# Loading the first batch's q in two token halves, one ahead of v and one behind it

## The chip, the cores and the metric

The kernel runs on one core of one Trainium2 chip. The metric is device time in microseconds of one execution, the median over several; lower is better. Two kernels are compared by a ratio, with a 95% interval, in the same rounds. It isn't quite the ratio of the medians that are quoted beside it.

In the lines of the profile PE is TensorE and PEld its weight loads, DVE is VectorE, ACT ScalarE and POOL GpSimd. SPq is the queue on which SyncE issues transfers (q1 in the DMA views), POOLq that of GpSimd (q0). Of the tiles, `wi` is the weight w_in, `qb` is q cast to bf16, `xT` the transposed attention output and `vc` the scaled v.

## The reference

Linear attention on random features for 8 batches of 8 heads, 576 tokens, head size 64, followed by a gated feed-forward layer:

```
phi(x) = exp(x @ omega.T - |x|^2/2 - max) / sqrt(m)      # m = 128 features
kv  = sum over tokens of phi(k) v ;  z = sum of phi(k)
att = (phi(q) kv) / (phi(q) z + 1e-6)                    # per batch and head
x   = att as (8*576) x 512
h   = x @ w_in                                           # 512 x 2048
out = (h * clip(h + 3, 0, 6) / 6) @ w_out                # 2048 x 512
```

## The kernel before

The kernel lists its operations with estimated durations, orders them with a list scheduler of its own while it is built, and emits the result. Batch 0 is special, for nothing can be overlapped with it. Its 512 main tokens are worked off in halves of 256, called A and B, so that the feed-forward layer can start on half A.

```
FIRST = [("k", 1), ("k", 0), ("q", 1), ("v", 0), ("v", 1), ("q", 0)]   # order of batch 0's loads; 1: main tokens, 0: leftover 64
W_GATE = [("vl", 0)]*2+[("v32", 1, 3)]*2     # what each quarter of w_in waits for before it is issued
...
# main loads: 4 rows to a partition, runs of 1024 B; 2 pairs of heads x 2 heads, 256 KB each
rows = src[b, 2 * m0 + hh:2 * m1 - 1 + hh:2, first:first + MAIN, :]
dma(..., rows.rearrange("m (p r) d -> p m (r d)", r=4), ..., 1024)
...
# w_in quarters go through GpSimd's queue, which converts f32 to bf16 on the way
...
def idle_work(count, each, gate):            # filler: matmuls on a constant tile while TensorE has nothing to do
    ...
def mm1_half(half, f):                       # feed-forward, first layer, for half A (0) or B (1) of batch 0
    ...  xT[0][:, c, 256 * half:256 * half + 256] ...  reads=[("xT", 0, c, half) ...] + [("wi", WI_OF[f])]
```

In the kernel before, "half A" is rows 0 and 1 of the four on each partition; q is loaded whole ahead of v. Whichever operation may run next is picked by priority within a tolerance (URGENT, FIT), and filler is placed where an engine would stand idle.

The softmax here doesn't subtract the row's maximum and nothing guards it: scores larger than these inputs give would overflow.

## Time and profile before

| | before |
|---|---|
| median of 4 runs | 324.05 us (323.71 to 324.29) |
| span of the profiled execution | 321.8 us |
| fillers on TensorE | 63, all before 17 us |
| first feed-forward matmul (half A) | 19.42 us |
| last quarter of w_in | issued 14.70 us, 10.1 us to landing: 24.8 us |

TensorE is the engine that sets the time; what it can still lose or gain is filler and idle time in the first 20 us. The prediction below shows the lines. The one to add is the stretch that follows, all engines (window, its length, then busy time and count of PE, PEld, DVE, ACT, POOL, then granted clock, DMA share and GB/s):

```profile
19.40:27.80 8.40, 8.40 (x95) 7.38 (x93) 6.94 (x19) 7.23 (x16) 5.02 (x7) 1.00 1.33 188
```

TensorE is busy for all 8.40 us, and 64 of its matmuls there are half A's feed-forward.

### The profile page before, as it was taken

The numbers are of one execution on the slowest core, as the hardware profiler recorded it, in microseconds if no ns is written. First come the engines' busy times: TensorE is split into PE (matmuls) and PEld (weight loads), VectorE is DVE, ScalarE is ACT, GpSimd is POOL, SyncE is SP. The second block draws the span as 40 slices with busy tenths as digits, with TensorE's granted clock in tenths as the row PEclk, the third lists the DMA queues.
The fourth block names the chain that finished last, engine by engine and source line by source line (L and its number), as shares of the span: only waits on it lengthen the run. The fifth ranks groups of instructions, "written<-read, shape, count | busy, mean of one in ns | idle before, by whom it ended". The sixth has DMA issues, their size and how long they took to land.

```text
span 321.8 us, 5873 instructions
## 1 busy us (share of the span) xinstructions
PE 317.0 (98%) x2236; PEld 174.8 (54%) x2236; DVE 209.0 (65%) x460; ACT 189.1 (59%) x385; POOL 76.8 (24%) x107
## 2 busy tenths in 40 slices
PE   8999999999999999999999999999999999999996
PEld 6789855455654544565555545555555444444443
DVE  4988985597787947995796478846866353433411
ACT  3996982596595516966775387647674254344400
POOL 2765171065040600730333022402020000000000
DMA  7999999999940999897829963998012201000024
GB/s 249 269 201 204 236 146 234 225 184 170 226 122 34 136 173 271 99 196 118 236 31 188 191 208 39 183 201 224 16 50 67 73 27 41 33 35 33 33 67 98
DMA packets 91532, 44.79 MB, mean 139 GB/s; under 512 B 58096, under 2 KB 87024, under 8 KB 91504
## 3 DMA queue, kind: packets, MB, share of 16 engines
q1 hardware_dynamic: 64288, 31.31, 42.1%
q0 software_dynamic: 26512, 12.46, 31.4%
q10 hardware_dynamic: 704, 0.66, 0.6%
q8 instruction: 18, 0.29, 0.4%
q14 instruction: 10, 0.08, 0.1%
HBM read 36.73 MB, written 9.44 MB: 143 GB/s over the span
## 4 chain that ended last, share of the span: by engine, by line
PE 94%; DVE 4%; POOL 1%; issue 0%; ACT 0%; POOLq 0%; DVEq 0%
PE p L917 39%; PE p L859 34%; PE p L656 5%; PE p L639 4%; PE p L884 4%; PE p L791 3%; PE p L763 2%; DVE mx L648 2%; PE p L466 2%; PE p L429 1%; PE p L765 1%; POOL vc L750 0%; DVE vc L750 0%; DVE vcl L679 0%; DVE gT L895 0%
## 5 line engine op out<-in xcount | busy, mean ns | idle before, releaser
L917 PE MATMUL p<-wo,gT 128*128 128x512 bf16 (+2 forms) x592 | 141.0, 373 | 0.3 <-DVE qT L418 0.3
L867 DVE SCALAR_TENSOR_TENSOR gT<-tsb,p 128x512 bf16<-128x512 bf16 x128 | 86.8, 685 | 56.7 <-ACT tsb L865 56.1
L865 ACT ACTIVATE tsb<-p 128x512 bf16<-128x512 f32 x128 | 76.3, 601 | 71.1 <-PE p L859 70.6
L859 PE MATMUL p<-xT,wi 128*128 128x512 bf16 x448 | 107.3, 379 | 0.0
L917 PEld LDWEIGHTS p<-wo,gT 128*128 128x128 bf16 x592 | 56.1, 98 | 57.5 <-DVE qT L418 0.5
L859 PEld LDWEIGHTS p<-xT,wi 128*128 128x128 bf16 x448 | 42.6, 98 | 45.4
L648 DVE TENSOR_REDUCE mx<-kp 128x4 f32<-128x512 bf16 x72 | 46.7, 674 | 9.7 <-ACT kp L645 9.4
L645 ACT ACTIVATE kp<-p 128x512 bf16<-128x512 f32 x72 | 40.0, 619 | 15.1 <-PE p L639 15.1
L660 ACT ACTIVATE qpT<-p 128x512 bf16<-128x512 f32 (+1 forms) x80 | 41.4, 575 | 4.8 <-PE p L656 4.6
L750 POOL TENSOR_TENSOR vc<-v,cc 128x512 bf16<-128x512 f32 x22 | 23.4, 1064 | 36.3 <-DVE cc L746 27.0
L807 DVE TENSOR_TENSOR xb<-p,rec 128x384 bf16<-128x384 f32 (+1 forms) x64 | 28.5, 477 | 0.0
L639 PE MATMUL p<-om,kT 128*128 128x256 bf16 x144 | 23.0, 273 | 0.0
L656 PE MATMUL p<-qT,om 128*128 128x512 bf16 (+1 forms) x80 | 22.8, 358 | 0.0
L418 DVE COPY osb<-p 128x512 f32<-128x512 f32 (+2 forms) x12 | 7.8, 647 | 22.7 <-PE p L917 22.7
L417 ACT COPY osb<-p 128x512 f32<-128x512 f32 x25 | 14.8, 591 | 11.3 <-PE p L917 11.3
L500 POOL DMA_DIRECT2D k<-in_k_dram x12 | 9.1, 767 | 41.9 <-PE p L859 33.7
L639 PEld LDWEIGHTS p<-om,kT 128*128 128x128 bf16 x144 | 13.8, 98 | 9.7
L791 PEld LDWEIGHTS p<-kvz,qpT 128*128 128x128 bf16 x312 | 13.5, 98 | 5.8 <-ACT qpT L660 0.2
L859 PE MATMUL p<-xS,wi 128*128 128x512 bf16 x64 | 16.4, 379 | 0.0
L884 PE MATMUL p<-xT,wi 128*128 128x256 bf16 x128 | 15.9, 272 | 0.0
L763 PEld LDWEIGHTS p<-vc,kp 128*128 128x128 bf16 x256 | 11.9, 98 | 6.1 <-POOL vc L750 0.4
L791 PE MATMUL p<-kvz,qpT 128*128 128x65 bf16 x312 | 14.8, 194 | 0.0
(69 smaller groups left out, 215.9 us busy)
## 6 DMA issues: line engine op xcount, KB each, us to landing
out_dram<-osb SPq DMA_DIRECT2D x32, 256.0 KB, 2.6
v<-in_v_dram SPq DMA_DIRECT2D x14, 512.0 KB, 5.3
wi<-in_moe_w_in_dram POOLq DMA_DIRECT2D x4, 512.0 KB, 8.3
k<-in_k_dram POOLq DMA_DIRECT2D x8, 256.0 KB, 5.1
k<-in_q_dram POOLq DMA_DIRECT2D x8, 256.0 KB, 6.2
wo<-in_moe_w_out_dram POOLq DMA_DIRECT2D x4, 512.0 KB, 12.8
kb<-in_k_dram POOLq DMA_DIRECT2D x6, 256.0 KB, 5.3
qb<-in_q_dram POOLq DMA_DIRECT2D x6, 256.0 KB, 7.6
```

Source lines behind the costliest of these rows:

```text
L639: ins = E.matmul(ring.t[vK.slot][:, 256 * i:256 * i + 256], kT[:, 2 * u + i, :], om[:].rearrange("d t m -> d (t m)"), start=True, stop=True)
L645: op("ACT", actt(512), lambda E, u=u, vK=vK: E.activation(kp[pb][:, 4 * u:4 * u + 4, :].rearrange("p c m -> p (c m)"), ring.t[vK.slot], AF ...
L648: op("DVE", dvet(512), lambda E, u=u: E.reduce_max(mx[pb][:, 4 * u:4 * u + 4], kp[pb][:, 4 * u:4 * u + 4, :], axis=AX.X), pos(u) + 0.03, r ...
L656: op("PE", mmt(n), lambda E, vQ=vQ, lh=lh: E.matmul(ring.t[vQ.slot][:, 0:n], om[:, lh, :], src, start=True, stop=True), p + 0.045 * lh, re ...
L660: op("ACT", actt(n), lambda E, vQ=vQ, lh=lh: E.activation(dst(lh), ring.t[vQ.slot][:, 0:n].rearrange("m (j t) -> m j t", t=128), AF.Exp, s ...
L791: ins = E.matmul(d[:, hh, i - i0, :], qpT[pb][:, o:o + 128], kvz[m][:, 65 * hh:65 * hh + 65], start=True, stop=True)
L807: op("DVE", dvet(128 * n), lambda E: E.tensor_tensor(xv(i0, i1), psum()[:, :, :, 0:64], rbc, ALU.mult), t + 0.01, reads=[vn, ("rec", ru)], ...
L859: ins = E.matmul(ring.t[vh.slot], wi[:, c, 128 * f:128 * f + 128], xv[:, c, :], start=(c == 0), stop=(c == NJ - 1))
L865: op("ACT", actt(512), lambda E: E.activation(tsb[tu][:], ring.t[vh.slot], AF.Relu, bias=0.5, scale=1.0 / 6.0), t - 0.1, reads=[vh], write ...
L867: op("DVE", dvet(512), lambda E: E.scalar_tensor_tensor(gT[gu][:, f, :], tsb[tu][:], 1.0, ring.t[vh.slot], ALU.min, ALU.mult), t - 0.1, re ...
L884: ins = E.matmul(ring.t[vh.slot][:, 256 * g:256 * g + 256], wi[:, c, 128 * (f + g):128 * (f + g) + 128], xT[0][:, c, 256 * half:256 * half ...
L917: ins = E.matmul(ring.t[vo.slot][:, 0:c1 - c0], gT[gu][:, f, 128 * tc:128 * tc + 128], wo[:, f, c0:c1], start=(f == 0), stop=(f == NF - 1))
```

## The change

Intent: v is needed by both halves, q's second half only later. So load q's half A, then v, then half B, and start the weights earlier. Half A becomes tokens 0 to 255, with two rows to a partition (runs of 512 B instead of 1024 B). A gate is what a load waits for before it is issued: `("v32", 1, 3)` is the last main transfer of v, `("q32", 1, 3, 0)` the last one of q's half A, `("vl", 0)` v's leftover tokens.

```diff
-URGENT = 0.8
-FIT = 0.05
+URGENT = 0.5
+FIT = 0.1
@@ rule for filler
-(0.02 if idle[0][0] < 8.0 else idle[0][1].occ)
+(0.02 if idle[0][0] < 4.8 else 0.2 if idle[0][0] < 8.0 else idle[0][1].occ)
@@
-    FIRST = [("k", 1), ("k", 0), ("q", 1), ("v", 0), ("v", 1), ("q", 0)]
+    FIRST = [("k", 1), ("k", 0), ("q", 1), ("v", 0), ("v", 1), ("q", 2), ("q", 0)]
+    QB_GATE = [("v32", 1, 3)]
-    W_GATE = [("vl", 0)]*2+[("v32", 1, 3)]*2
+    W_GATE = [("q32", 1, 3, 0)] * 4
@@ estimate of a load: by its run length
-packet=50.0 if run == 1024 else 18.0
+packet={1024: 50.0, 512: 36.0, 256: 18.0}[run]
@@
+        def q_half(half):
+            for m0, m1 in HALVES:
+                for hh in range(2):
...
+                    rows = q[0, 2 * m0 + hh:2 * m1 - 1 + hh:2, 256 * half:256 * half + 256, :]
+                    dma(..., rows.rearrange("m (p r) d -> p m (r d)", r=2),
+                        65536 * (m1 - m0), [("q32", hh, m, half) ...], QB_GATE if half else [], base["q"], 512)
@@ scheduler's estimates for GpSimd's two scalings of v
-{"POOL": 0.62 ...  {"POOL": 1.2 ...
+{"POOL": 0.72 ...  {"POOL": 1.32 ...
```

The rows of the first output block are permuted to match, in runs of the same 2 KB.

More of the change, by code (lines that the diff above doesn't have):

```diff
@@ L186, in schedule @@
                 m = min([x[0] for x in cand] + [1e9])
-                if idle and (not cand or idle[0][0] + (0.02 if idle[0][0] < 8.0 else idle[0][1].occ) <= m):
+                if idle and (not cand or idle[0][0] + (0.02 if idle[0][0] < 4.8 else 0.2 if idle[0][0] < 8.0 else idle[0][1].occ) <= m):
                     if idle[0][0] > IDLE_UNTIL:
@@ L498, in dma @@
             e = "POOL" if cast else eng[turn_of[0]] if turn_of[0] < len(eng) else "SP"
-            op(e, n * (0.74 if b == 0 else 0.8) * (1.0 if run == 1024 else 1.5) / 262144.0,
+            op(e, n * (0.74 if b == 0 else 0.8) * {1024: 1.0, 512: 1.1, 256: 1.5}[run] / 262144.0,
                lambda E: E.dma_start(dst, src), prio + 0.001 * turn_of[0], reads=gate + (free if cast else []), writes=keys,
                group="d" + part + ("c" if cast else "") + (str(pb) if b and part != "v" else ""), inc=16, lat=1.0,
-               name="%s.%d" % (part, b), issue=0.85 if cast else 0.47, packet=50.0 if run == 1024 else 18.0)
+               name="%s.%d" % (part, b), issue=0.85 if cast else 0.47, packet={1024: 50.0, 512: 36.0, 256: 18.0}[run])
             turn_of[0] += 1
@@ L538, in lefts @@
                     gates[t], base[t], 256)
+        def q_half(half):
+            for m0, m1 in HALVES:
+                for hh in range(2):
+                    d = q32[:, NP:, :].rearrange("p (m h s r) d -> p m h s (r d)", h=2, s=2, r=2)
+                    rows = q[0, 2 * m0 + hh:2 * m1 - 1 + hh:2, 256 * half:256 * half + 256, :]
+                    dma("q%d%d%d" % (hh, m0, half), d[:, m0:m1, hh, half, :], rows.rearrange("m (p r) d -> p m (r d)", r=2),
+                        65536 * (m1 - m0), [("q32", hh, m, half) for m in range(m0, m1)], QB_GATE if half else [], base["q"], 512)
         tensors = {"k": (k, KB[pb] if b else k32), "q": (q, QB[pb] if b else q32), "v": (v, v32)}
         for t, part in FIRST if b == 0 else REST:
-            (mains if part else lefts)(t, *tensors[t])
+            if t == "q" and b == 0 and part:
+                q_half(part - 1)
+            else:
+                (mains if part else lefts)(t, *tensors[t])
     def attention(b):
@@ L615, in attention @@
                     cast("q", nm, 512, pairs(qb)[:, 2 * m0:2 * m1, s, :], pairs(q32)[:, 2 * m0:2 * m1, s, :],
-                         main_keys("q", range(m0, m1)), dbl, 0)
+                         [k_ + (s,) for k_ in main_keys("q", range(m0, m1))], dbl, 0)
                     turns("q", nm, dbl, alts(qT, s, m0, m1), qb, 0)
@@ L678, in attention @@
             p0 = 64 * hh
-            op(EV_V if b else V0, {"POOL": 0.62, "DVE": dvet(260)}, lambda E, hh=hh, p0=p0: E.tensor_tensor(
+            op(EV_V if b else V0, {"POOL": 0.72, "DVE": dvet(260)}, lambda E, hh=hh, p0=p0: E.tensor_tensor(
                 vcl[pb][p0:p0 + 64, :, 65 * hh:65 * hh + 65], vl[pb][p0:p0 + 64, :, :],
@@ L749, in pair @@
         vcm = vc[u2][:].rearrange("p (c e) -> p c e", e=65)
-        op(EV_V if b else V0, {"POOL": 1.2, "DVE": dvet(512)}, lambda E: E.tensor_tensor(
+        op(EV_V if b else V0, {"POOL": 1.32, "DVE": dvet(512)}, lambda E: E.tensor_tensor(
             vcm[:, :, 0:D], v32[:, m, :, :], cbc, ALU.mult),
@@ L928, in mm2 @@
             if blk < 8:
-                dsts = [(0, 128, out[blk * S:blk * S + MAIN, :].rearrange("(p r) e -> r p e", r=4)[tc])]
+                rows = out[blk * S:blk * S + MAIN, :]
+                dsts = [(0, 128, rows[256 * (tc // 2):256 * (tc // 2) + 256, :].rearrange("(p r) e -> r p e", r=2)[tc % 2] if blk == 0 else
+                         rows.rearrange("(p r) e -> r p e", r=4)[tc])]
             else:
```

## The prediction

> **What bounds the kernel now.** I read the page first, then the waits of TensorE, then the first 28 us by window and in order of time, since everything in the change that isn't a cost estimate of the kernel's own instruction scheduler belongs to the first batch.
>
> ```profile
> span 321.8 us, 5873 instructions
> PE 317.0 (98%) x2236; PEld 174.8 (54%) x2236; DVE 209.0 (65%) x460; ACT 189.1 (59%) x385; POOL 76.8 (24%) x107
> PE 94%; DVE 4%; POOL 1%; issue 0%; ACT 0%; POOLq 0%; DVEq 0%
> ```
>
> TensorE sets the time: 94% of the chain that ended last. But some of its work is filler. The group of line 466 is matmuls on a constant tile that keep TensorE awake while there is nothing to do:
>
> ```profile
> L466 PE MATMUL p<-fill x63: 272/273/421, 1.3 to 16.9; 128*128 128x256 bf16 x63
> ```
>
> The column of durations overlaps from one matmul to the next; the pace is better read from a row of 23 of them in order of time:
>
> ```profile
> 10.36 2.49 PEld L466 LDWEIGHTS p<-fill 128*128 128x128 bf16 x23
> ```
>
> 2.49 / 23 = 0.108 us each, so 63 fillers are 6.8 us that no output needs, all before 16.9 us. By window of that group alone (the first number after the window is its length, then busy time and count):
>
> ```profile
> 0.00:8.60 8.60, 5.46 (x23) 3.11 (x23) 1.00 0.81 256
> 8.60:19.40 10.80, 5.39 (x40) 3.60 (x40) 1.00 1.19 246
> 19.40:27.80 8.40, 0.00 (x0) 0.00 (x0) 1.00 1.33 188
> ```
>
> 40 x 0.108 = 4.3 us of filler stand between 8.6 and 19.4 us. At 19.42 us the first matmul of the feed-forward part starts (line 884, half A: the first 256 tokens of batch 0). From there on TensorE is dense, so the kernel ends earlier by about as much as that start is brought forward, if no new hole opens behind it. This stretch of 10.8 us is the only place where the change can earn. What sets its length:
>
> ```profile
> 8.60:19.40 10.80, 10.72 (x133) 8.27 (x132) 9.93 (x27) 9.94 (x26) 7.87 (x11) 1.00 1.19 246
> 8.70 2.96 DVE mx L648 x5
> 11.91 0.68 DVE vc L750
> 12.59 1.19 DVE mx L648 x2
> 13.77 0.60 DVE vc L750
> 14.37 1.08 DVE mx L648 x2
> 15.50 0.62 POOL qb L418
> 16.20 1.37 POOL vc L750
> 17.61 0.43 PE p L763 x8
> 19.42 0.38 PE L884 MATMUL p<-xT,wi 128*128 128x256 bf16 x2
> ```
>
> The first row is all engines in that stretch: VectorE is busy for 9.93 us and ScalarE for 9.94 us of 10.8 (each 92%), GpSimd for 7.87 us. The DMA is full too (share 1.19). The next rows are the chain of waits: maxima of k on VectorE, the scaling of v, two more maxima, another scaling; then GpSimd, which casts q of half B (15.50) before it can scale the last pair's v (16.20), and only then TensorE multiplies k and v. So three engines are nearly full, and v itself is waited for only at one point: the second v transfer lands about 11.8 us (issued about 6.1 us, 5.7 us to landing), just when VectorE has finished five maxima (11.66) and two reciprocals. v arrives no later than VectorE is ready for it, within 0.2 us.
>
> **What the Trainium skill says.** (1) DMA: Bandwidth & Descriptors, section "Queues, rings and completion order": each of the 16 engines goes round robin between the queues that have work, a packet at a time. In the trace v travels alone until about 12.5 us, so before the change there is almost no sharing between v and the wi weights to see; after it there will be. (2) The same page, section "Specifications", gives 512 B as the smallest transfer for full rate. The trace agrees in direction: the q transfers of 256 KB in 1024 B runs land 0.74 to 0.8 us apart (340 KB/us), the 128 KB of vl in 256 B runs take 0.57 us more (225 KB/us). The change's 512 B runs are at the edge. (3) The same page, section "Anatomy of one DMA", says a semaphore wait happens on the issuing sequencer before dispatch. So a gated q transfer holds back whatever is issued behind it on the SP queue. No gate stands on SP's early loads now, so this trace doesn't show it. (4) TensorE: Matmul & The Clock Gate says an idle window of about 3.4 us halves the clock. The granted clock here is 1.00 throughout, thanks to the filler; the changed rule for filler between 4.8 and 8 us thins it but leaves no such gap.
>
> **The change part by part.**
> Transfers: q's four transfers of 256 KB before v become four of 128 KB. Before: 4 x 0.76 = 3.05 us. After, at an estimated 300 KB/us between the two rates above: 4 x 0.43 = 1.7 us. So vl and v are brought forward by about 1.3 us: the second v transfer from 11.8 to about 10.5 us.
> Weights: now two wi pieces wait for vl (GpSimd idle 1.1 us, issue at 10.62) and two for the last v transfer (13.90). All four will wait for q's first half, which should land about 7.0 + 1.7 = 8.4 to 8.7 us. They take about 0.8 us of GpSimd each to issue (3.25 us for four, from the rows at 10.62 and 13.90, same sum as before), and land 6.6 to 10 us after issue. Data starts some 2 us after issue, so at 10.5 instead of 12.6 us. wi is therefore up to 2 us earlier: the first piece near 15.5 instead of 10.62 + 6.6 = 17.2 us. It then runs beside v's third and fourth transfers. A wi packet took about 0.10 us in the trace and a v packet of 1024 B about 0.05 us, so by round robin v gets one third of the rate: these two may land near 12.8 and 15 instead of 12.6 and 13.6 us. That hurts little: their scaling ran at 15.86 and 16.20 us.
> Half B of q: its casts (ScalarE 0.67 us at 12.28, GpSimd 0.62 us at 15.50) and the two copies after its transposes (ScalarE 1.08 us at 16.63) leave the stretch: 1.75 us of ScalarE, 0.62 us of GpSimd just ahead of its v scaling. They aren't saved: they come back behind 19.4 us, where ScalarE is busy for 7.23 and VectorE for 6.94 us of 8.4, so 1.2 and 1.5 us are free there.
> The start of half A: VectorE's 9.93 us don't shrink, since its maxima, reciprocals, scalings and divisions are all still needed. With v early and in better order it can use its 0.87 us of idle time, and ScalarE's relief of 1.75 us shortens the steps from kv to the transposed x; GpSimd's v scaling moves up by about 0.6 us. I take 1.0 us as the forward move of 19.42, with 0.3 to 1.8 as its spread.
> Given back: half B's 1.75 us on ScalarE need more than the 1.2 us free there, and its q lands late (below): 0.2 us, and a further 0.1 us either way as the scheduler shuffles the instructions of later batches (URGENT, FIT and the new GpSimd costs reorder the rest too). Output rows of the first block keep 2 KB each: 0.
> Sum: 324.18 - 1.0 + 0.2 = 323.4 us; as the weights' earlier landing also brings the next batch's k forward, I lean a little lower: 323.2 us.
>
> **The rivals.**
> Rival 1, the late half takes the place of the early one. q's second half waits for v's last transfer (about 13 to 15 us) and then shares with wi. With 512 B packets against wi's, its 512 KB may move at about 100 KB/us: 5 us, plus 2 us to start, so it lands at 19 to 22 us. Its cast, transpose, copy, projection, exponent, product, division and transpose take about 5 us in a row, so half B's x is ready about 24 to 27 us. Half A's 64 matmuls run until 27.8 us now and to about 26.8 us then. For: this is tight. Against: half B's group starts a little later than its first need, and other work of TensorE (of the next batch) can fill in. If it bites, TensorE idles 1 to 2 us and the time is 324 to 325.5 us.
> Rival 2, nothing moves: VectorE at 92% in the stretch is the bound, v only looks late, and the early v finds VectorE in its maxima (8.70 to 11.66). For: the row of VectorE. Against: the filler and ScalarE's load. Then the time stays at 323.9 to 324.4 us.
> Rival 3, all three engines profit: with the weights 2 us earlier, v 1.3 us earlier and half B out of the way, half A starts 2 us or more earlier and the filler falls by 20. Then 321.5 to 322.3 us. Against it: VectorE alone needs 9.9 us after the first k has come.
> Rival 4, wi chokes v more than the round-robin estimate says, also the second transfer: then half A starts later and the time is 325 us.
>
> **Range and chances.** My middle, 323.2 us, is 0.3% under before. All the filler between 8.6 and 19.4 us is 4.3 us, 1.3% of the time: even the best case is inside 2% (6.5 us). A loss of 6.5 us would need half of the first batch's loads to come late. So within 2% has 0.98, 0.01 for each side. The range 321.7 to 324.7 us holds the middle, rival 2, most of rivals 1 and 3.
>
> **What would show it right or wrong.** Right: first line-884 matmul at 18 to 19 us instead of 19.42; about 50 to 57 fillers instead of 63; the first v scaling near 11 us instead of 11.89; wi issues from about 8.5 us on; no q cast of half B before 15 us. Wrong: a TensorE wait of over 0.5 us between 24 and 30 us on half B's x (rival 1); the start of line 884 within 0.2 us of 19.42 (rival 2); the first v scaling later than 12 us (rival 4); a granted clock under 1.00.

## The result, and the profile after

The changed kernel takes 325.89 us (325.68 to 326.29, 4 runs) against 324.05 us before: ratio 1.0059, 95% interval 1.0042 to 1.0077. It is slower, clear of noise, by about 1.9 us. That is inside the 2% that was forecast with 0.98, but outside the range of 321.7 to 324.7 us, and on the wrong side of the time before.

The page after:

```profile
span 324.1 us, 5845 instructions
PE 315.3 (97%) x2204; PEld 175.0 (54%) x2238; DVE 211.3 (65%) x465; ACT 188.6 (58%) x380; POOL 75.1 (23%) x107
PE 87%; DMA 5%; ACT 3%; SPq 2%; issue 1%; DVE 1%
```

Before, 94% of the chain was TensorE and no DMA was in it. Now TensorE has 87%, and DMA and the SP queue stand in its place. (2204 matmuls against 2238 weight loads: 34 matmul records are missing from this trace. Two more weight loads than before are the two more fillers.) The chain of waits says which transfer it is (start, duration, what):

```profile
6.90 5.11 DMA v<-in_v_dram
...
13.48 10.90 DMA q<-in_q_dram
...
24.40 0.63 ACT qb L418
...
25.07 0.40 PE p L430 x4
```

The last transfer of v is issued at 6.90 us and lands at 12.01. That opens the gate of q's half B; its fourth transfer is issued at 13.48 and takes 10.90 us to land, at 24.38. Then ScalarE casts it, and TensorE transposes it at 25.07. The same in order of time, with TensorE's waits in square brackets:

```profile
8.69 3.19 POOL L477 DMA_DIRECT2D wi<-in_moe_w_in_dram  x4 [0.51 <-DMA q<-in_q_dram]
...
11.50 0.69 DVE L763 TENSOR_TENSOR vc<-v,cc 128x512 bf16<-128x512 f32 x1
...
17.93 0.60 PE L897 MATMUL p<-xT,wi 128*128 128x256 bf16 x4
...
20.32 0.62 POOL L419 CAST qb<-q 128x512 bf16<-128x512 f32 x1 [3.65 <-DMA q<-in_q_dram]
...
21.00 0.40 PE L430 MATMUL p<-ident,qb 128*128 128x128 bf16 x4 [0.70 <-POOL qb L419]
...
24.40 0.62 ACT L418 CAST qb<-q 128x512 bf16<-128x512 f32 x1 [1.40 <-DMA q<-in_q_dram]
...
25.07 0.40 PE L430 MATMUL p<-ident,qb 128*128 128x128 bf16 x4 [1.16 <-ACT qb L418]
```

The first feed-forward matmul did come forward, from 19.42 to 17.93 us. But TensorE then waits twice for a cast of half B. GpSimd and ScalarE had waited themselves: the two casts start as q lands. TensorE's waits between 19 and 35 us in total:

```profile
PEld p L430 <- ACT qb L418: 1.3, 1, 1.3
PE p L430 <- ACT qb L418: 1.2, 1, 1.2
PEld p L430 <- POOL qb L419: 1.0, 1, 1.0
PE p L430 <- POOL qb L419: 0.7, 1, 0.7
PEld p L897 <- DVE xT L419: 0.6, 1, 0.6
PE p L897 <- DVE xT L419: 0.4, 1, 0.4
```

(Columns: who waited for whom, us in total, times, longest.) In the same window the kernel before has no such row for a cast of q; its only one of TensorE is a weight load's 0.2 us. The sum of the matmul rows is 2.3 us. By window, all engines, and then the filler alone in the first of the two:

```profile
8.60:19.40 10.80, 10.52 (x134) 8.61 (x133) 10.04 (x27) 8.96 (x24) 7.43 (x9) 1.00 1.20 247
19.40:27.80 8.40, 6.54 (x74) 5.24 (x72) 4.69 (x14) 5.18 (x11) 5.58 (x8) 1.00 1.36 203
```

```profile
8.60:19.40 10.80, 5.89 (x42) 3.89 (x42) 1.00 1.20 247
```

In the second stretch TensorE falls from 8.40 to 6.54 us busy: 1.9 us, the size of the whole loss. In the first it has gained nothing: 42 fillers where there were 40. Although half A starts 1.5 us earlier, no more useful work gets done before 19.4 us, since half B's transposes and projections have left that stretch. VectorE is at 10.04 us of 10.8 there (9.93 before); it is as full as before.

Why is half B so late? The DMA view, between half B's first issue (12.02 us) and its first data, and then while it moves (queue, packets, MB, share of 16 engines):

```profile
q0 software_dynamic: 533, 0.53, 122.6%
```

```profile
q0 software_dynamic: 1015, 1.01, 84.7%
q1 hardware_dynamic: 1012, 0.49, 35.1%
```

The first line is the window 12.7 to 15.3 us. Only the weights' queue q0 moves; SP's queue q1 moves nothing, although half B's transfers were issued on it from 12.02 us on. Its first data comes at 15.61 us, 3.6 us after the issue. With no other transfer moving, the same transfer needed 1.0 us for this (experiment 9: issued 12.25 us, first data 13.27), so about 2.6 us are held back. The second view is 16 to 23 us: the two queues send the same number of packets, 1015 and 1012. One has packets of 1 KB, the other of 512 B. So half B gets 0.49 MB in 7 us, 70 KB/us, where half A's transfers, of the same size, took 0.45 us for 128 KB ahead of v (284 KB/us).

### The profile page after: what moved, and what is told of

Read it like the earlier page. It is cut to its first block, busy times and chain, and to the rows that moved or that the text cites. A ratio compares the mean times of both kernels' runs of the same rounds, so it can differ in the third digit from the quotient of the medians.

```text
span 324.1 us, 5845 instructions
## 1 busy us (share of the span) xinstructions
PE 315.3 (97%) x2204; PEld 175.0 (54%) x2238; DVE 211.3 (65%) x465; ACT 188.6 (58%) x380; POOL 75.1 (23%) x107
## 4 chain that ended last, share of the span: by engine, by line
PE 87%; DMA 5%; ACT 3%; SPq 2%; issue 1%; DVE 1%
PE p L930 38%; PE p L872 32%; PE p L652 4%; PE p L669 4%; DMA q<-in_q_dram 3%; PE p L804 3%; PE p L897 3%; SPq L501 2%; PE p L776 2%; DMA v<-in_v_dram 2%; ACT qpT L673 1%; PE p L430 1%; ACT tsb L878 1%; ACT kp L658 1%; PE p L778 0%
## 5 line engine op out<-in xcount | busy, mean ns | idle before, releaser
L930 PE MATMUL p<-wo,gT 128*128 128x512 bf16 (+2 forms) x576 | 139.6, 373 | 0.9 <-issue 0.2
L872 PE MATMUL p<-xT,wi 128*128 128x512 bf16 x434 | 105.6, 379 | 0.8
L763 POOL TENSOR_TENSOR vc<-v,cc 128x512 bf16<-128x512 f32 x20 | 21.5, 1073 | 29.8 <-DVE cc L759 23.5
## 6 DMA issues: line engine op xcount, KB each, us to landing
wo<-in_moe_w_out_dram POOLq DMA_DIRECT2D x4, 512.0 KB, 12.7
```

The costliest lines, as they stand in the source:

```text
L872: ins = E.matmul(ring.t[vh.slot], wi[:, c, 128 * f:128 * f + 128], xv[:, c, :], start=(c == 0), stop=(c == NJ - 1))
L930: ins = E.matmul(ring.t[vo.slot][:, 0:c1 - c0], gT[gu][:, f, 128 * tc:128 * tc + 128], wo[:, f, c0:c1], start=(f == 0), stop=(f == NF - 1))
```

## The experiments

Eleven kernels ran, in three groups. All gave correct results. In the diffs, "A" is the changed kernel and "B" the kernel before.

### 1. The gate removed: ungated

```diff
 A
-    QB_GATE = [("v32", 1, 3)]
+    QB_GATE = []
```

> The changed kernel, with q's second half no longer gated on v's last transfer, so that it stands directly behind v on the same queue. Theory (late q): the changed kernel loses because q's second half is issued at 12.0 us, when the weights already have the DMA engines, and lands at 18.4 to 24.4 us; TensorE, in order, waits for its casts (0.7 us at 20.4, 1.2 us at 23.9). Without the gate its data should start at about 12 us and land by 14 to 18 us, the two waits should go, and the time fall from 325.9 to 323.5 to 324.7 us. Rival (scheduler settings or 512 B runs cost it): the time stays at 325.5 to 326.2 us.

Measured: 323.62 us, ratio to before 0.9997 (0.9983 to 1.0011). One line takes back the whole loss. SP issues half B right behind v:

```profile
7.63 2.01 SPq L501 DMA_DIRECT2D q<-in_q_dram  x4
```

It lands at 12.6 to 13.9 us, the weights' first data waiting until it is nearly through. No wait of TensorE of 0.2 us or more is left between 19 and 35 us, and the stretch is full again:

```profile
8.60:19.40 10.80, 10.58 (x134) 8.47 (x133) 9.89 (x28) 8.57 (x22) 8.10 (x10) 1.00 1.20 252
19.40:27.80 8.40, 8.40 (x95) 7.27 (x93) 7.08 (x20) 6.98 (x15) 5.36 (x8) 1.00 1.38 200
```

So late q is the cause. The order of issue changes in one more place: q's leftover tokens now go out behind half B, at 9.68 and 10.48 us, and land at 17.6 and 19.4 us instead of 12.3 and 12.6, at no visible cost. The run shows a second thing too: with everything in time and half A starting at 18.0 us, the kernel still isn't faster than before. Fillers in the first stretch are 41 (40 before), VectorE 9.89 us (9.93), ScalarE 8.57 us (9.94). The relief went to ScalarE; VectorE, as full as it, got none.

### 2. The same loads, an order that expects them late: order_truth

```diff
 A
-packet={1024: 50.0, 512: 36.0, 256: 18.0}[run]
+packet={1024: 50.0, 512: 28.0, 256: 18.0}[run]
-inc=16, lat=1.0,
+inc=16, lat=1.8 if run == 512 and gate else 1.0,
```

> The changed kernel with the same loads and gates, but its scheduler is told that q's second half moves slower and lands later (18.5, 20.3, 22.0, 23.7 us, close to what was measured), so that it places half B's instructions later in TensorE's fixed order. Theory (late data as such): both the last weights (25.6 us) and half B of q come late, so there is too little other work to fill in: 325 to 326.5 us. Rival (only the order was wrong, since the scheduler expected 17.5 to 21.8 us): the waits at 20.4 and 23.9 us vanish and the time falls to 324.5 us or less.

Measured: 325.28 us, ratio 1.0043 (1.0031 to 1.0056). The two waits on casts shrink to one of 0.2 us, but others come up in the window from 24 to 32 us:

```profile
PE p L430 <- DVE xb L820: 0.6, 1, 0.6
PE p L897 <- ACT xT L418: 0.5, 1, 0.5
...
PEld p L897 <- DMA wi<-in_moe_w_in_dram: 0.2, 1, 0.2
```

By the ratios some 0.5 us of the 1.9 us (1.0059 less 1.0043 is 0.16%) was the wrong order, but the two intervals overlap, so this share isn't shown. The greater part of the loss stays (1.0031 at least). TensorE is busy again for 8.27 us of the stretch 19.4 to 27.8 us, and the hole has moved behind it, where the kernel before has 7.20 us of 7.20:

```profile
27.80:35.00 7.20, 5.94 (x67) 4.83 (x65) 4.84 (x13) 4.61 (x10) 2.99 (x4) 1.00 1.34 252
```

Half B's last q lands at 24.68 us and the last weights at 25.89 us there, and TensorE then waits for half B's x. This order, which knows about the lateness, moves the hole and doesn't fill it; other orders weren't tried.

### 3. The settings alone on the old loads: params_only

The diff is that of the change for URGENT, FIT, the filler rule and the two GpSimd estimates, on B.

> The kernel before with only the changed scheduler settings (URGENT, FIT, the rule for filler, the two GpSimd costs), all loads as before. Theory (late q): within 0.5 us of the kernel before, 323.7 to 324.7 us. Rival (the settings reorder things for the worse): 325.3 us or more.

Measured: 325.11 us, ratio 1.0037 (1.0024 to 1.005). A miss: I expected no effect, and it came close to the rival's 325.3. The half A start is at 20.8 us. TensorE waits 1.1 us for the scaling of v on VectorE, and one of these scalings ran beside one on GpSimd:

```profile
16.96 1.04 POOL L750 TENSOR_TENSOR vc<-v,cc 128x512 bf16<-128x512 f32 x1 [0.51 <-DVE rec L803]
16.98 1.56 DVE L750 TENSOR_TENSOR vc<-v,cc 128x512 bf16<-128x512 f32 x1
```

VectorE needs 0.70 us (median) for this in the kernel before, and 1.56 us here: it began 0.02 us after GpSimd's and ended 0.54 us after it. In the kernel of experiment 4 it is the other way round: VectorE's began 0.06 us earlier and took 0.69 us, and GpSimd's took 1.54 instead of 1.04 us. So these two hardly run side by side. The settings do it by reordering, so their effect depends on the loads; experiments 4, 5, 6 and 11 show that.

### 4. Both halves ahead of v: q_all_first

```diff
 A
-FIRST = [..., ("q", 1), ("v", 0), ("v", 1), ("q", 2), ("q", 0)]
+FIRST = [..., ("q", 1), ("q", 2), ("v", 0), ("v", 1), ("q", 0)]
-QB_GATE = [("v32", 1, 3)]
+QB_GATE = []
-W_GATE = [("q32", 1, 3, 0)] * 4
+W_GATE = [("vl", 0)]*2+[("v32", 1, 3)]*2
```

> The changed kernel, with both halves of q in front of v in 512 B runs, no gate on the second, and the weights gated as before the change. It has the new row layout, the 512 B runs and the new settings, and nothing late. Theory (late q): 323.8 to 324.8 us, as before. Rival (layout and short runs cost it): 325.3 us or more; the eight q transfers would then take clearly over 3.05 us (0.45 us each is 3.6 us).

Measured: 323.66 us, ratio 0.9992 (0.998 to 1.0005), just under the range expected. The new layout, the 512 B runs and the new settings together cost nothing. The eight transfers land 0.43 to 0.50 us apart, about as expected. So neither the short runs alone nor the settings as such made the changed kernel slow.

### 5. The changed loads with the old settings: loads_only

The settings of experiment 3 set back on A.

> The changed kernel with the scheduler settings of the kernel before (URGENT, FIT, filler rule, GpSimd costs); loads, gate and layout as changed. Theory (late q): still about 2 us slower than before, 325.4 to 327 us, with TensorE waits on the casts of half B. Rival (the settings are at fault, since they alone cost 1.1 us on the old loads): 324.8 us or less.

Measured: 326.56 us (325.73 to 326.79), ratio 1.0073 (1.0061 to 1.0086). The loss is in the loads and their gate, and the new settings didn't cause it. (They look 0.14% better here, but the intervals overlap.) TensorE waits 1.0 and 0.5 us for casts of half B.

### 6. Neither gate nor new settings: ungated_oldset

> The changed kernel with neither the gate nor the new settings: q in halves, the second directly behind v, weights early. Theory (late q): 323.3 to 324.5 us, as the ungated kernel with the new settings (323.62). If the settings had a cost of their own of 1.1 us whatever the loads, this would be 322.5 us or less.

Measured: 323.96 us, ratio 1.0001 (0.9989 to 1.0013). Together with ungated: on these loads the settings are worth 0.04%, nothing.

### 7. A gate that opens earlier: gate_mid

```diff
 A
-    QB_GATE = [("v32", 1, 3)]
+    QB_GATE = [("v32", 1, 1)]
```

> The changed kernel with q's second half gated on v's second transfer (lands 10.4 us) instead of the fourth (12.0 us), so that it is issued some 1.6 us earlier and its data can follow v without a gap. Theory (what counts is whether its data get in ahead of the weights'): the second half lands by 14 to 16 us, no wait of TensorE over 0.5 us on half B between 20 and 26 us, about 323.6 to 324.6 us, although the scheduler still expects it at 17.5 to 21.8 us. Rival (any gated transfer goes to the back of the weights): lands at 17 to 24 us, 325 to 326 us.

Measured: 325.02 us, ratio 1.0039 (1.0026 to 1.0052). My theory's version missed and its rival held. Half B is issued from 10.58 us, 1.4 us earlier than in the changed kernel and while v's last two transfers still move. Yet its four transfers land at 17.6 to 23.4 us, about 1 us earlier and nowhere near 14 to 16. What the earlier issue couldn't change is that GpSimd had issued the weights at 8.8 us. Its first data comes at 14.21 us, again 3.6 us after the issue, although its own queue was still moving until 11.98 us. So it isn't enough to be issued before v has landed. The ungated run has both sides on one queue: half B's fourth transfer (issue from 9.17 to 9.64 us) took 4.7 us to land, and the next one, a leftover of half the size (9.68 to 10.43 us), took 7.9 us. GpSimd's issue of the first weights lasted from 8.88 to 9.82 us. What fits all these runs is that the issue must be finished before that of the weights.

### 8. The weights early, nothing else: before_wi_early

```diff
 B
-    W_GATE = [("vl", 0)]*2+[("v32", 1, 3)]*2
+    W_GATE = [("q32", 1, 3)]*4
```

> The kernel before with only the gate of the weights moved: all four wait for q's last transfer (lands 9.75 us) instead of vl and v's last. It asks whether early weights are worth anything by themselves. Theory (the DMA is full until 25 us and the order only trades): the last weights land within 0.5 us of 24.8 us and the time stays within 0.7 us of before. Rival (weights limit half A): wi up to 1 us earlier, time 323.3 us or less.

Measured: 324.18 us (323.43 to 324.94), ratio 1.0006 (0.9992 to 1.002). Issuing the weights' last quarter at 12.44 instead of 14.70 us made it land at 24.55 instead of 24.8 us. The DMA is full to then and the order only trades one transfer for another. Early weights are worth nothing by themselves.

### 9. Gate kept, weights behind it too: gated_wi_late

```diff
 A
-    W_GATE = [("q32", 1, 3, 0)] * 4
+    W_GATE = [("v32", 1, 3)] * 4
```

> The changed kernel with its gate on q's second half kept, but the weights gated on the same event, v's last transfer. Theory (q is late because it is issued behind the weights' first piece, not because of the gate as such): q's second half now starts within about 2 us of its issue and its four transfers land by about 18 us instead of 18.4 to 24.4; the weights pay: their last piece lands 26.5 to 27.7 us instead of 25.6, half A runs out of weights, and the time is 324.5 to 326 us. Rival (the gate alone delays q): q lands after 20 us again.

Measured: 327.59 us (327.22 to 329.24), ratio 1.0138 (1.0113 to 1.0163): slower than expected. But it is the cleanest look at the mechanism. Here GpSimd issues the weights' first quarter at 12.54 us, between half B's first transfer (12.25) and the others. The first of these lines is that first transfer, the second the third one, issued at about 13.84 us (count, size, us to landing):

```profile
q<-in_q_dram SPq DMA_DIRECT2D x1, 128.0 KB, 2.4
```

```profile
q<-in_q_dram SPq DMA_DIRECT2D x1, 128.0 KB, 7.0
```

Same size, same queue, same gate: 2.4 us when issued ahead of the weights, 7.0 us when issued behind them. The one just behind (12.68 us), with only the first ahead of it on its own queue, took 6.2 us and is the fairer comparison. My expectation that all four would land by 18 us was wrong, since only one of them got ahead. By its number the rival came true for the last two (20.8 and 22.6 us), but its reason, that the gate alone delays q, falls with the first. TensorE waits for half B's casts again, and longer:

```profile
PE p L430 <- POOL qb L419: 1.6, 1, 1.6
PE p L430 <- ACT qb L418: 0.6, 1, 0.6
```

### 10. A try for a faster version: ungated_truth

```diff
 ungated
-packet={1024: 50.0, 512: 36.0, 256: 18.0}[run]
+packet={1024: 50.0, 512: 600.0, 256: 18.0}[run]
```

> The ungated kernel, its scheduler told that the short-run transfers keep nearly the whole rate beside the weights, so that it expects q's second half at 13.4 to 14.8 us (measured 12.6 to 13.9) instead of 14.4 to 18.7. A try for a version faster than both kernels: half B's work can be placed earlier into fillers. Theory (filler goes only if the first batch's other engines have room): 323.0 to 324.0 us, within 0.3% of before. Rival (order is what holds it back): 322.5 us or less.

Measured: 323.23 us (322.78 to 323.91), ratio 0.9983 (0.997 to 0.9995). The scheduler now expects half B about when it lands and gives it an earlier place. It beats the changed kernel clearly (by 0.8% across the two groups of rounds) and the kernel before by 0.17%; the interval just excludes 1, which one of eleven comparisons may do by chance. It has the lowest ratio found, but its interval overlaps those of experiments 1 and 4. The rival's 322.5 us wasn't reached.

### 11. Layout and short runs alone: q_all_first_oldset

The kernel of experiment 4 with the old settings.

> The kernel with q's two halves both ahead of v (new layout, 512 B runs) and the settings of the kernel before: layout and short runs alone. Theory: 323.5 to 324.8 us, no cost beyond 0.6 us for q's landing later by some 0.7 us. If the new settings had made up for a cost of the layout in the run with both (323.66), this would be 325 us or more.

Measured: 324.10 us, ratio 1.001 (0.9998 to 1.0023). The layout with 512 B runs costs 0.1% by the ratio, 0.23% at most by the interval, and perhaps nothing. Of the settings: +0.37% on the old loads (3), -0.18% here (4 against 11), -0.14% on the gated loads (5 against the change), -0.04% ungated (1 against 6). Only the first is clear of noise; the intervals of the other pairs overlap. No value of their own is shown; they pick another order.

### What the experiments leave

The lateness of half B is shown as the cause (1), and being issued behind the weights as its reason (7 and 9). The order that did not expect it may account for a quarter (2); that isn't clear of noise. Why the ungated kernels gain so little from v's earlier arrival was looked at in their traces alone: VectorE's 9.9 us of 10.8 fits, but no run took work off VectorE to prove it, and in ungated_truth VectorE is busy for 10.36 us of that stretch, with 41 fillers still, so 9.9 us is no ceiling. A rival is untested: the last weights land no earlier there (25.3 us in ungated, 24.8 before), and in ungated_oldset TensorE waits 1.0 us for weights. How the DMA engines hold back a later transfer for some 2.6 us before they alternate stays open; the runs show that they do.

## Why the prediction was wrong

- Transfers ahead of v: right. v was to come 1.3 us earlier; its second transfer landed at 10.44 us (10.5 forecast). The estimate of 300 KB/us for 512 B runs measured as 284.
- Weights issued from about 8.5 us: right (8.69). That their data would start at 10.5 us and slow v's third and fourth transfers to 12.8 and 15 us was wrong: they landed at 11.20 and 12.01 us. The weights' first packet came at 11.47 us only, when v was nearly through. I had applied the even sharing to the transfer that it doesn't hurt.
- Half A's start: right in its own number, 17.93 us instead of 18.4, within the stated spread of 0.3 to 1.8 us. But the step "the kernel ends earlier by about as much as that start is brought forward" failed. Its condition, "if no new hole opens behind it", wasn't met; and in the ungated run, where no hole opens and half A starts at 18.0 us, the kernel is no faster either. Filler was to fall from 63 to between 50 and 57; it rose to 65 (in the stretch from 40 to 42). When work is taken out of a stretch to start something sooner, the start is no measure of the gain; the useful work done by a given moment is. Rival 2 gave a reason that fits: VectorE stayed at 10.04 us.
- "Given back: ... 0.2 us": this is the term that was mis-sized. TensorE lost 1.9 us in the stretch behind (8.40 to 6.54 us). The mechanism was rival 1, which I described and priced at 324 to 325.5 us; the measured 325.89 us is above even that. Its sizes: 100 KB/us estimated, 70 measured; 2 us to start, 3.6 measured; landing at 19 to 22 us, 18.4 to 24.4 measured. My own sharing rule gave less than 100: a packet from each queue in turn, 0.10 us for one of the weights and about 0.03 us for one of 512 B (at the 300 KB/us that I took), is 16 x 0.5 KB in 0.13 us, about 60 KB/us (an estimate from the prediction's figures). Its sign, a wait of over 0.5 us on half B's x, came one step earlier: 1.2 us on the cast of half B's q, ended at 25.07 us.
- "Other work of TensorE can fill in" was the argument against rival 1, and it was wrong twice: the order is fixed by the scheduler's estimates (17.5 to 21.8 us for half B), so work behind the wait may not step in; and where the order knew, the hole opened later (experiment 2). My range was said to hold most of rival 1; it held 324 to 324.7 of 324 to 325.5 us, less than half of a rival that I had called tight.
- The Trainium skill, DMA: Bandwidth & Descriptors, section "Queues, rings and completion order", says that the engines go round robin by packet. The trace agrees in the counts once both queues move (1015 packets to 1012), but between half B's issue and its first data, 3.6 us later, it doesn't show it; about 2.6 us of that isn't the transfer's own start. The section "Anatomy of one DMA" has the semaphore wait on the issuing sequencer; what was behind the gate did stay unissued: half B's four transfers went out from 12.02 us, as v landed.

## What to carry to other kernels

When the DMA is full, moving a transfer back isn't free: find what was issued ahead of it on any queue and count its rate in packets, with the sizes of both sides. A gate on a transfer also sets its place behind whatever is issued meanwhile, so prefer a place in the queue to a gate. And where each engine's order is fixed from estimated arrivals, a late transfer stops everything behind its first consumer; measure landings and put them in the estimates.

## What the Trainium skill lacked or had wrong

- DMA: Bandwidth & Descriptors, "Queues, rings and completion order": round robin by packet holds here in the long run (1015 against 1012 packets in 7 us), so short packets get fewer bytes (0.49 against 1.01 MB). A packet of the profile is one run of 512 B or 1 KB; the page's is several descriptors. It doesn't tell of the start: with the weights already issued on GpSimd's queue, the transfer issued on SP at 12.02 us had no packet in 12.7 to 15.3 us, while q0 sent 533; with the engines idle its first data came 1.0 us after the issue. Issued 0.3 us ahead of the weights, such a transfer landed in 2.4 us; issued behind, in 6.2 and 7.0 us.
- The same page, "Specifications", has 512 B as the smallest transfer for line rate. Here 128 KB in 512 B runs took 0.45 us (284 KB/us) and 256 KB in 1024 B runs about 0.76 us (340 KB/us), with SP's queue alone on the engines: 512 B is a sixth short of 1 KB (the transfers are also half as large, which no run separates). The page does tell of a fixed cost per packet elsewhere, but works it out for 256 B only.
